# Channel mixing over the 896 tokens of two batches: pieces of 512 and 384 columns in place of two of 448

## Chip, cores and metric

One core of one Trainium2 chip. The metric is the device time of one execution in microseconds (us); shown is the median of several runs. The engines are TensorE (PE; its weight loads are listed apart as PEld), VectorE (DVE), ScalarE (ACT), GpSimd (POOL) and SyncE (SP), which issues most of the transfers.

## What is computed

The reference chains three parts on 2 batches of 448 tokens: attention (12 heads of 64), a gated feed-forward part that mixes tokens, and a last part that mixes tokens and then channels. The change is in the channel mixing of the last part (and in the tiles that lead to it):

```python
xt = x.transpose(0, 2, 1)                        # x: (2, 448, 768)
h = np.maximum(xt @ w_tok1, 0.0) @ w_tok2
u = x + h.transpose(0, 2, 1)
h2 = np.maximum(u @ w_ch1, 0.0) @ w_ch2          # w_ch1: 768 x 1536, w_ch2: 1536 x 768
return (u + h2).astype(np.float32)
```

## The kernel before

Activations are kept with channels on the 128 partitions and tokens along the columns, so that 768 channels are 6 tiles (`ND`) and the 1536 hidden channels are 12 (`NC`). Every number is held as a pair hi + lo of a rounded float32 (`F32R`) and its remainder. A product takes three matmuls, hi·hi, hi·lo and lo·hi (`three`), and each matmul has a weight load of its own.

The code records operations with the buffers that they read and write (`Plan.op`). `Plan.schedule` then simulates the engines with rough costs (one matmul over 448 columns is a slot of 203 ns, `SLOT`), picks at each step the operation that can start first, and so sets the order on each engine. `BUFS` says how many buffers each tag has; a buffer is given back when its last user is planned. One recorded PE operation is up to 6 matmuls (`mm`, `step=6`).

The last part goes in these steps:

- `tok1_unit`: 4 units, matmuls over 384 columns.
- `tok2_unit`: for batch `b` and channel tile `d` 6 matmuls over 448 columns into a bank (tag `gm`). DVE adds the bank to the residual (line L972), ACT casts the sum to hi (L350), DVE subtracts for lo (L367). The result `U[b][d]` is one tile `[128, 2, 448]` of tag `x` (12 buffers) that holds hi and lo of one batch.
- `ch1_unit`: for each of 12 hidden tiles `f`, first the 18 matmuls of batch 0 over 448 columns, then the 18 of batch 1, into the two banks of one `sc` buffer (there are 2 such buffers). `relu_split` reads both banks: ACT takes max(·, 0) as hi (L935), DVE the remainder as lo (L938).
- `ch2_unit`: for each of 6 output tiles `d` 36 matmuls over 448 columns for batch 0 and 36 for batch 1, each in a bank of its own. POOL has made hi + lo of `U[b][d]` ahead of time (`whole`, L891), DVE adds the bank to it (L1011), and a transfer writes it out (L1018). The last piece is cut into two halves, one issued by SP, the other by ACT.

All matmuls of these steps but the transposes are issued by one line, L274 in `mm`. The weights of each step come as 64-bit numbers through SP's queue (2 buffers of tag `r`), are turned into float32 by ACT and DVE (3 buffers of tag `t`), and are split into hi and lo by a cast (ACT, DVE, or POOL at L355) and a subtraction (DVE L367 or POOL L368) in buffers of tag `a`. There are 21 of these; in `ch2_unit` 18 hold the hidden tiles `f` from 3 on, and 3 hold weights, one `d` at a time.

Of the kernel before, what the change touches and what calls it, by code (L numbers as in the profile page):

```python
# [17 lines left out]
NP = H // 2  # L18
DM = H * D
ND = DM // 128  # L20
DF = 512
NF = DF // 128
ST = 112
NS = S // ST
NR = 3
# [42 lines left out]
    "ch1": (-24, 4),  # L68
    "ch2": (74, 5),
}  # L70
BUFS = {"x": 12, "v": 3, "q": 6, "a": 21, "r": 2, "t": 3, "h": 13, "p": 6, "gm": 4, "sc": 2, "sm": 4}
SLOT = 203.0
LAT = 140.0
EARLY = 72.0
# [16 lines left out]
        return self.ap[i]  # L91


class Op:
    __slots__ = ("ways", "key", "seq", "deps", "bufs", "new", "eng", "fn", "start", "end", "nbytes", "nwait")


class Plan:
# [5 lines left out]
    def op(self, ways, key, r=(), w=(), nbytes=0):  # L104

        o = Op()
        o.ways, o.key, o.seq, o.nbytes = ways, key, len(self.ops), nbytes
        o.deps, o.new = [], []
        o.bufs = list(dict.fromkeys(list(r) + list(w)))
        for b in o.bufs:  # L110
            if b.users == 0 and b.ap is None:
                o.new.append(b)
            b.users += 1
            write = any(b is x for x in w)
            if write or b.psum:
                o.deps += b.last_writers + b.readers
                if write:
                    b.last_writers, b.readers = [o], []
                else:
                    b.readers = [o]  # L120
            else:
                o.deps += b.last_writers
                b.readers.append(o)
        o.deps = list(dict.fromkeys(o.deps))
        self.ops.append(o)
        return o

    def schedule(self):
# [14 lines left out]
        for b in {b for o in ops for b in o.bufs if b.ap is not None and b.tag in free}:  # L143
            free[b.tag].pop()
        ready = defaultdict(list)

# [76 lines left out]
class Net:  # L223
    def __init__(self, tc, io, pool, ps, anycap=False):
        self.tc, self.nc, self.io, self.pool, self.ps, self.anycap = tc, tc.nc, io, pool, ps, anycap
        self.plan = Plan()
        self.key = 0.0


    def buf(self, tag, shape, dtype=F32):  # L230
# [351 lines left out]
    def normalise(self, n, A):  # L582
# [30 lines left out]
        for h, rows in ((0, LO), (1, UP)):  # L613
# [7 lines left out]
                1,  # L621
                kn,
            )
        x = self.buf("x", [128, 2, S], F32R)
# [55 lines left out]
    def attention_anycap(self, n):  # L680
# [10 lines left out]
        for h, r in ((0, LO), (1, UP)):  # L691
            for m in range(NS):
# [69 lines left out]
        x = self.buf("x", [128, 2, S], F32R)  # L762
        self.split(S, lambda: x[:, 0], lambda: x[:, 1], lambda: xf.ap, [xf], [x], k0 + 8)
        return x

# [194 lines left out]
            )  # L960
        return hi, lo

    def tok2_unit(self, h1, w2, x2, d):
# [9 lines left out]
        u = self.buf("x", [128, 2, S], F32R)  # L973
        self.split(S, lambda: u[:, 0], lambda: u[:, 1], lambda: z.ap, [z], [u])
        return u


    def ch1_unit(self, ws, U, f):
        ps = self.bank2()
        for b in range(B):  # L980
            terms = []
            for d in range(ND):
                n, c = divmod(f % 2 * ND + d, 4)
                cs = slice(c * 128, (c + 1) * 128)
                terms += self.three(
                    lambda i, n=n, cs=cs: ws[n][:, i, cs], lambda i, d=d, b=b: U[b][d][:, i], [ws[n], U[b][d]]
                )
            self.mm(ps, lambda b=b: ps[:, b, :S], terms, 1)
        hi, lo = (self.buf("q" if f < 3 else "a", [128, 2, S], F32R) for _ in range(2))
        self.relu_split(2 * S, (hi, lambda: hi.ap), (lo, lambda: lo.ap), ps, lambda: ps[:, :, :S])  # L990
        return [[hi, lo]] * B, lambda i, b: (hi, lo)[i][:, b]

    def ch2_unit(self, ws, h2, U, d):
        nc, io = self.nc, self.io
        for b in range(B):
            ps = self.bank()
            terms = []
            for f in range(NC):
                cs = slice(f % 4 * 128, (f % 4 + 1) * 128)
                terms += self.three(  # L1000
                    lambda i, f=f, cs=cs: ws[f // 4][:, i, cs], lambda i, f=f, b=b: h2[f][1](i, b), [ws[f // 4], *h2[f][0][b]]
                )
            self.mm(ps, lambda ps=ps: ps[:, :S], terms, 1)
            u = U[b][d]
            cuts = [slice(0, S // 2), slice(S // 2, S)] if (b, d) == (B - 1, ND - 1) else [slice(0, S)]
            o = [self.h([128, cs.stop - cs.start]) for cs in cuts]
            for i, cs in enumerate(cuts):
                self.whole(o[i], u, cs)
                self.dve(
                    cs.stop - cs.start,  # L1010
                    lambda o=o[i], ps=ps, cs=cs: nc.vector.tensor_tensor(out=o.ap, in0=ps[:, cs], in1=o.ap, op=ALU.add),  # L1011
                    [ps, o[i]],
                    [o[i]],
                )
            for i, (cs, out) in enumerate(zip(cuts, (nc.sync, nc.scalar))):
                self.load(
                    128 * (cs.stop - cs.start) * 4,
                    lambda o=o[i], b=b, cs=cs, out=out: out.dma_start(  # L1018
                        out=io["out"][b, d * 128 : (d + 1) * 128, cs], in_=o.ap
                    ),  # L1020
                    [],
                    [o[i]],
                    on="ACT" if i else "SP",
                )

    def run(self):
# [42 lines left out]
        for b in range(B):  # L1069
            h1[b] = stage([lambda t=t: self.tok1_unit(b, tr[b], xr, w1, t) for t in range(NT)], 4)  # L1070
        for b in range(B):
            U[b] = stage([lambda d=d: self.tok2_unit(h1[b], w2, x2[b], d) for d in range(ND)], 1.1)

        c1 = {}

# [84 lines left out]
def build(arrays):  # L1160
    import concourse.bacc as bacc

    nc = bacc.Bacc("TRN2", target_bir_lowering=False, num_devices=1)
    io = {
        n: nc.dram_tensor(f"{n}_in", a.shape, mybir.dt.from_np(a.dtype), kind="ExternalInput").ap()
        for n, a in arrays.items()
    }
    io["out"] = nc.dram_tensor("out_t", (B, DM, S), F32, kind="ExternalOutput").ap()
    with tile.TileContext(nc) as tc:
        program(tc, io)  # L1170
    return nc
# [10 lines left out]
```

## Time and profile before

| | |
|---|---|
| median of 3 runs | 442.62 us (442.54 to 443.59) |
| the profiled execution's own time | 444.11 us |
| its span in the trace | 442.3 us |
| PE busy | 427.0 us (97%) |
| DVE, ACT busy | 264.8 us (60%), 265.7 us (60%) |
| POOL busy | 105.5 us (24%) |
| first matmul of `ch1_unit` | at 257.44 us |
| first matmul of `ch2_unit` | at 346.73 us |
| matmuls in each of the two steps | 432 |

The profile is of one execution. Its own time is 1.8 us longer than the span that the trace covers. Matmuls overlap in the trace: one begins while the one before it still drains, so the time that a matmul takes from its engine is the distance from its start to the next one's start, not its duration.

### The profile page before, as it was taken

The page shows a single profiled execution, that of the slowest core. Times are in us where ns is not written, and L with a number is a line of the kernel's source. Part 1 is how long each engine was busy: PE and PEld are TensorE (multiplying, and loading weights), DVE is VectorE, ACT ScalarE, POOL GpSimd, SP SyncE. Part 2 cuts the span into 40 slices and gives each one's busy share as a digit, 9 for nine tenths or more (in the row PEclk, how much of TensorE's full clock was granted, in tenths as well). Part 3 has the DMA queues.
Part 4 walks back from the last instruction along what each step waited for, and adds up shares of the span by engine and source line. Part 5 has one row for each costly group of instructions (what it writes and reads, how often), then busy time and mean ns, then how long its engine had stood idle before and what let it go on. Part 6 is the DMA issues. An engine that isn't in the chain of part 4 may idle for free.

```text
span 442.3 us, 5467 instructions
## 1 busy us (share of the span) xinstructions
PE 427.0 (97%) x2050; PEld 350.2 (79%) x2050; DVE 264.8 (60%) x413; ACT 265.7 (60%) x386; POOL 105.5 (24%) x105
## 2 busy tenths in 40 slices
PE   8997989998999999999999999999999999999994
PEld 5553546566775889999999999999999999999993
DVE  4899989776665765896546899655202242344210
ACT  6998899999999567525537825775404333353100
POOL 0333342320100141567005473111010011011100
PEclk9999989999999999999999999999999999999998
DMA  7535546352120402202402105444201223533010
GB/s 266 207 125 173 176 128 210 102 157 88 47 70 2 142 5 92 83 1 99 139 1 96 48 1 168 164 144 142 96 0 49 96 90 116 184 117 123 34 44 29
DMA packets 14867, 44.84 MB, mean 101 GB/s; under 512 B 1904, under 2 KB 4208, under 8 KB 14832
## 3 DMA queue, kind: packets, MB, share of 16 engines
q1 hardware_dynamic: 14688, 44.30, 30.4%
q8 instruction: 18, 0.29, 0.3%
q14 instruction: 17, 0.14, 0.1%
q10 hardware_dynamic: 144, 0.11, 0.1%
HBM read 41.65 MB, written 2.75 MB: 100 GB/s over the span
## 4 chain that ended last, share of the span: by engine, by line
PE 78%; ACT 12%; DVE 7%; issue 2%; POOL 0%; DVEq 0%; POOLq 0%; ACTq 0%
PE gm L274 48%; PE sc L274 20%; PE gm L572 5%; ACT a L514 3%; ACT a L522 3%; PE sc L540 2%; DVE t L449 1%; DVE q L367 1%; PE sc L905 1%; ACT L768 1%; DVE t L438 1%; DVE h L592 1%; PE gm L561 1%; PE sc L342 1%; DVE h L616 1%
## 5 line engine op out<-in xcount | busy, mean ns | idle before, releaser
L274 PE MATMUL gm<-a,a 128*128 128x448 f32 (+1 forms) x556 | 115.2, 363 | 0.0
L274 PEld LDWEIGHTS gm<-a,a 128*128 128x128 f32 x556 | 102.8, 188 | 8.4
L274 PE MATMUL sc<-x,a 128*128 128x448 f32 x432 | 89.4, 368 | 0.0
L274 PEld LDWEIGHTS sc<-x,a 128*128 128x128 f32 x432 | 81.1, 188 | 8.2
L572 PE MATMUL gm<-a,v 128*128 128x448 f32 x144 | 61.8, 558 | 4.8 <-ACT a L522 2.8
L427 DVE SCALAR_TENSOR_TENSOR t<-r,t 128x512 int32<-128x512 int32 (+1 forms) x52 | 40.5, 782 | 30.1 <-ACT t L420 27.9
L274 PE MATMUL gm<-q,a 128*128 128x448 f32 x268 | 57.3, 367 | 0.0
L407 ACT ACTIVATE t<-r 128x512 uint16<-128x512 uint16 (+1 forms) x52 | 40.5, 784 | 25.3 <-DVE a L367 20.8
L396 ACT ACTIVATE r<-r 128x512 f32<-128x512 f32 (+1 forms) x58 | 38.9, 670 | 25.3 <-DMA r<-ch_in 23.1
L274 PEld LDWEIGHTS gm<-q,a 128*128 128x128 f32 x268 | 50.3, 188 | 4.7
L572 PEld LDWEIGHTS gm<-a,v 128*128 128x128 f32 x144 | 25.5, 191 | 29.6 <-issue 20.6
L368 POOL TENSOR_TENSOR a<-t,a 128x512 fp32r<-128x512 f32 x21 | 29.4, 1402 | 77.6 <-DVE a L351 73.7
L355 POOL TENSOR_SCALAR a<-t 128x512 fp32r<-128x512 f32 x19 | 12.2, 644 | 127.3 <-PE gm L274 71.9
L420 ACT ACTIVATE t<-r 128x512 f16<-128x512 f32 (+1 forms) x52 | 40.3, 774 | 0.0
L367 DVE TENSOR_TENSOR a<-t,a 128x512 fp32r<-128x512 f32 x35 | 24.6, 704 | 20.7 <-POOL a L355 20.1
L522 ACT ACTIVATE a<-a,acap 128x896 f32<-128x896 f32 x36 | 36.5, 1043 | 0.1
L514 ACT ACTIVATE a<-sc,qs 128x896 f32<-128x896 f32 x36 | 35.1, 1004 | 2.2 <-PE sc L540 2.2
L891 POOL TENSOR_TENSOR h<-x 128x448 f32<-128x448 f32 (+1 forms) x25 | 33.5, 1368 | 9.0 <-PE gm L274 6.1
L274 PE MATMUL gm<-x,a 128*128 128x448 f32 x144 | 31.0, 372 | 0.0
L938 DVE SCALAR_TENSOR_TENSOR a<-sc,a 128x896 fp32r<-128x896 f32 x9 | 9.8, 1092 | 33.3 <-ACT a L935 33.3
L274 PEld LDWEIGHTS gm<-x,a 128*128 128x128 f32 x144 | 27.1, 188 | 3.3 <-issue 1.0
L935 ACT ACTIVATE a<-sc 128x896 fp32r<-128x896 f32 x9 | 8.3, 920 | 32.7 <-PE sc L274 32.7
(97 smaller groups left out, 492.5 us busy)
## 6 DMA issues: line engine op xcount, KB each, us to landing
r<-ch_in SPq DMA_DIRECT2D x36, 512.0 KB, 3.3
r<-w_in_in SPq DMA_DIRECT2D x12, 512.0 KB, 3.9
q<-qk_in SPq DMA_DIRECT2D x11, 544.0 KB, 4.3
v<-va_in SPq DMA_DIRECT2D x12, 288.0 KB, 4.4
r<-w_out_in SPq DMA_DIRECT2D x6, 512.0 KB, 3.4
out_t<-h SPq DMA_DIRECT2D x11, 224.0 KB, 1.9
r<-tok_in SPq DMA_DIRECT2D x2, 512.0 KB, 3.4
t<-w_sg_in SPq DMA_DIRECT2D x4, 224.0 KB, 2.5
```

Of the source, the lines that this page charges most:

```text
L274: self.nc.tensor.matmul(view(), l, rr, start=(i + m == 0), stop=(i + m == n - 1))
L355: lambda: nc.gpsimd.tensor_scalar(out(), src(), 1.0, 0.0, ALU.mult, ALU.add),
L367: "DVE": ("DVE", n / 0.96 + 155, lambda: nc.vector.tensor_tensor(**args()), not psum),
L368: "POOL": ("POOL", n * 2.3 + 60, lambda: nc.gpsimd.tensor_tensor(**args()), True),
L396: lambda: nc.scalar.activation(raw[:, :, 1].bitcast(F32), raw[:, :, 1].bitcast(F32), AF.Copy, scale=2.0**-112),
L407: lambda: nc.scalar.activation(t.ap.bitcast(U16)[:, 0::2], raw.ap.rearrange("p n t -> p (n t)").bitcast(U16)[:, 1::4], AF.Copy, scale=2.0* ...
L420: lambda: nc.scalar.activation(t.ap.bitcast(F16)[:, 1::2], raw[:, :, 1].bitcast(F32), AF.Copy),
L427: lambda: nc.vector.scalar_tensor_tensor(out=t.ap, in0=raw[:, :, 1], scalar=3, in1=t.ap, op0=ALU.logical_shift_left, op1=ALU.bitwise_or),
L514: lambda: nc.scalar.activation(te.ap, sc[:, 0:nn, :S], AF.Tanh, scale=self.qs),
L522: lambda: nc.scalar.activation(te.ap, te.ap, AF.Exp, scale=self.acap),
L572: nc.tensor.matmul(A[h][:, :S], V[:, 3 * j + h : 3 * j + h + 2].rearrange("p c d -> p (c d)"), E[j][:, h], start=(j == 0), stop=(j == 2),)
L891: lambda: self.nc.gpsimd.tensor_tensor(out=out.ap, in0=parts(0), in1=parts(1), op=ALU.add),
```

## The change

The 896 tokens of both batches are one row of columns, cut into pieces of 512 and 384 (`WIDE`) where it was cut at the batches into 448 and 448. For this `U[0][d]` and `U[1][d]` become two parts (`Part`) of one tile `[128, 2, 896]` of tag `x`, of which there are 6 in place of 12; the x tiles of the attention, which have the same tag, are held in the same way. The first piece takes all of batch 0 and 64 columns of batch 1, so every matmul of `ch1_unit` in it needs both batches. The two pieces of `ch1_unit` lie next to each other in the two banks, and the hidden tiles are `[128, 896]`. The output in memory is `(768, 896)` in place of `(2, 768, 448)`.

```diff
+WIDE = slice(0, 512), slice(512, 2 * S)
...
-BUFS = {"x": 12, "v": 3, "q": 6, "a": 21, "r": 2, "t": 3, "h": 13, "p": 6, "gm": 4, "sc": 2, "sm": 4}
+BUFS = {"x": 6, "v": 3, "q": 6, "a": 21, "r": 2, "t": 3, "h": 13, "p": 6, "gm": 4, "sc": 2, "sm": 4}
...
+class Part(Buf):
+    def __init__(self, whole, cs):
+        self.whole, self.cs, self.tag, self.psum = whole, cs, None, False
...
+    @property
+    def ap(self):
+        return self.whole.ap[:, :, self.cs]
...
+    def x_part(self, d, b):
+        if b == 0:
+            self.both[d] = self.buf("x", [128, 2, B * S], F32R)
+        return Part(self.both[d], slice(b * S, (b + 1) * S))
...
     def ch1_unit(self, ws, U, f):
         ps = self.bank2()
-        for b in range(B):
+        for m, ts in enumerate(WIDE):
             terms = []
             for d in range(ND):
...
-                    lambda i, n=n, cs=cs: ws[n][:, i, cs], lambda i, d=d, b=b: U[b][d][:, i], [ws[n], U[b][d]]
-                )
-            self.mm(ps, lambda b=b: ps[:, b, :S], terms, 1)
-        hi, lo = (self.buf("q" if f < 3 else "a", [128, 2, S], F32R) for _ in range(2))
...
+                    lambda i, d=d, ts=ts: U[0][d].whole[:, i, ts],
+                    [ws[n], U[0][d], U[1][d]],
+                )
+            size = ts.stop - ts.start
+            self.mm(ps, lambda m=m, size=size: ps[:, m, :size], terms, size / S)
+        hi, lo = (self.buf("q" if f < 3 else "a", [128, 2 * S], F32R) for _ in range(2))
+        src = lambda: ps.ap.rearrange("p m n -> p (m n)")[:, : 2 * S]
...
     def ch2_unit(self, ws, h2, U, d):
         nc, io = self.nc, self.io
-        for b in range(B):
+        for m, ts in enumerate(WIDE):
...
-                self.whole(o[i], u, cs)
+                at = slice(ts.start + cs.start, ts.start + cs.stop)
+                parts = lambda i, at=at: U[0][d].whole.ap.bitcast(F32)[:, i, at]
+                self.gps(
+                    size // n * 2.3 + 60,
+                    lambda o=o[i], parts=parts: nc.gpsimd.tensor_tensor(out=o.ap, in0=parts(0), in1=parts(1), op=ALU.add),
+                    [U[0][d], U[1][d]],
+                    [o[i]],
+                )
```

Up to the last matmul of `tok2_unit` the order of the instructions on PE is that of before. From there the planner's order differs. In the rows below the number behind a name tells buffers apart: `sc` is the bank pair of one hidden tile, `x` an input tile of `ch1_unit`, `a` a weight, `h` a residual or an output tile, and `gm` a bank of `tok2_unit`.

PE at the start of `ch1_unit`, before (x_2292 to x_2362 are batch 0, x_2372 to x_2425 batch 1):

```order
L274 MATMUL sc_2416<-x_2292,a_2155 128x448 x3
L274 MATMUL sc_2416<-x_2307,a_2155 128x448 x3
L274 MATMUL sc_2416<-x_2320,a_2155 128x448 x3
L274 MATMUL sc_2416<-x_2324,a_2155 128x448 x3
L274 MATMUL sc_2416<-x_2360,a_2175 128x448 x3
L274 MATMUL sc_2416<-x_2362,a_2175 128x448 x3
L274 MATMUL sc_2416<-x_2372,a_2155 128x448 x3
L274 MATMUL sc_2416<-x_2395,a_2155 128x448 x3
L274 MATMUL sc_2416<-x_2400,a_2155 128x448 x3
L274 MATMUL sc_2416<-x_2410,a_2155 128x448 x3
L274 MATMUL sc_2416<-x_2414,a_2175 128x448 x3
L274 MATMUL sc_2416<-x_2425,a_2175 128x448 x3
```

The same place in the changed kernel (x_2286 to x_2349 are the six tiles of both batches, sc_2399 is the first hidden tile and sc_2421 the second):

```order
L303 MATMUL sc_2399<-x_2286,a_2149 128x512 x3
L303 MATMUL sc_2399<-x_2301,a_2149 128x512 x3
L303 MATMUL sc_2399<-x_2313,a_2149 128x512 x3
L303 MATMUL sc_2399<-x_2324,a_2149 128x512 x3
L303 MATMUL sc_2421<-x_2286,a_2169 128x512 x3
L303 MATMUL sc_2421<-x_2301,a_2169 128x512 x3
L303 MATMUL sc_2421<-x_2313,a_2194 128x512 x3
L303 MATMUL sc_2421<-x_2324,a_2194 128x512 x3
L303 MATMUL sc_2399<-x_2337,a_2169 128x512 x3
L303 MATMUL sc_2399<-x_2349,a_2169 128x512 x3
L303 MATMUL sc_2399<-x_2286,a_2149 128x384 x3
L303 MATMUL sc_2399<-x_2301,a_2149 128x384 x3
```

The first hidden tile's matmuls on the channel tiles 4 and 5 (x_2337, x_2349) now stand behind twelve matmuls of the second hidden tile; before, all of the first hidden tile came first, batch by batch.

DVE at the end of `tok2_unit`, batch 1, before (the rows with `gm` are the sums, those with `x` the lo parts; the lo part of channel tile 0 of batch 1 stands one row above):

```order
L972 TENSOR_TENSOR h_1886<-gm_2350,h_1886 128x448
L972 TENSOR_TENSOR h_1891<-gm_2364,h_1891 128x448
L972 TENSOR_TENSOR h_1900<-gm_2376,h_1900 128x448
L972 TENSOR_TENSOR h_1934<-gm_2387,h_1934 128x448
L972 TENSOR_TENSOR h_1945<-gm_2402,h_1945 128x448
L367 TENSOR_TENSOR x_2395<-h_1886,x_2395 128x448
L367 TENSOR_TENSOR x_2400<-h_1891,x_2400 128x448
L367 TENSOR_TENSOR x_2410<-h_1900,x_2410 128x448
L367 TENSOR_TENSOR x_2414<-h_1934,x_2414 128x448
L367 TENSOR_TENSOR x_2425<-h_1945,x_2425 128x448
```

The same place in the changed kernel, from the lo part of channel tile 0 of batch 1 on:

```order
L396 TENSOR_TENSOR x_2286<-h_1858,x_2286 128x448
L1001 TENSOR_TENSOR h_1880<-gm_2342,h_1880 128x448
L1001 TENSOR_TENSOR h_1885<-gm_2355,h_1885 128x448
L1001 TENSOR_TENSOR h_1894<-gm_2366,h_1894 128x448
L396 TENSOR_TENSOR x_2301<-h_1880,x_2301 128x448
L396 TENSOR_TENSOR x_2313<-h_1885,x_2313 128x448
L396 TENSOR_TENSOR x_2324<-h_1894,x_2324 128x448
L1001 TENSOR_TENSOR h_1928<-gm_2378,h_1928 128x448
L1001 TENSOR_TENSOR h_1939<-gm_2390,h_1939 128x448
L396 TENSOR_TENSOR x_2337<-h_1928,x_2337 128x448
L396 TENSOR_TENSOR x_2349<-h_1939,x_2349 128x448
```

The lo parts of the channel tiles 1 to 3 moved ahead of the sums of 4 and 5.

POOL in this stretch, before (rows with `a` are lo parts of weights, rows `h<-x` the sums hi + lo for `ch2_unit`):

```order
L368 TENSOR_TENSOR a_2231<-t_2180,a_2231 128x512
L891 TENSOR_TENSOR h_2310<-x_2292 128x448
L368 TENSOR_TENSOR a_2334<-t_2271,a_2334 128x512
L891 TENSOR_TENSOR h_2357<-x_2307 128x448
L891 TENSOR_TENSOR h_2385<-x_2320 128x448
L891 TENSOR_TENSOR h_2397<-x_2372 128x448
L891 TENSOR_TENSOR h_2412<-x_2324 128x448
```

The same place in the changed kernel:

```order
L397 TENSOR_TENSOR a_2225<-t_2174,a_2225 128x512
L397 TENSOR_TENSOR a_2327<-t_2265,a_2327 128x512
L1046 TENSOR_TENSOR h_2374<-x_2286 128x512
L1046 TENSOR_TENSOR h_2386<-x_2286 128x384
L1046 TENSOR_TENSOR h_2408<-x_2301 128x512
L1046 TENSOR_TENSOR h_2418<-x_2301 128x384
L1046 TENSOR_TENSOR h_2460<-x_2313 128x512
```

The sums hi + lo begin one row later and now go tile by tile over both batches, 512 columns and then 384, where the first four of before were of x_2292, x_2307, x_2320 (batch 0) and x_2372 (batch 1). On SP the transfers stand in the order of before: for each output tile one output, one weight, one output, two weights.

## Rows read from the trace of the kernel before

**Rows 1.** The profile's page: busy time of each engine; relu_split's two groups.

```profile
PE 427.0 (97%) x2050; PEld 350.2 (79%) x2050; DVE 264.8 (60%) x413; ACT 265.7 (60%) x386; POOL 105.5 (24%) x105
...
L938 DVE SCALAR_TENSOR_TENSOR a<-sc,a 128x896 fp32r<-128x896 f32 x9 | 9.8, 1092 | 33.3 <-ACT a L935 33.3
...
L935 ACT ACTIVATE a<-sc 128x896 fp32r<-128x896 f32 x9 | 8.3, 920 | 32.7 <-PE sc L274 32.7
```

**Rows 2.** The chain that ended last, from 225 us: start, us, what.

```profile
257.61 89.28 PE sc L274 x432
346.89 89.29 PE gm L274 x432
```

**Rows 3.** Busy time by windows, ch1_unit and ch2_unit: window, its length, each engine's busy us.

```profile
257.44:346.73 89.29, 89.29 (x434) 81.08 (x433) 46.53 (x58) 41.35 (x61) 17.76 (x15) 1.00 0.31 101
346.73:436.00 89.27, 89.27 (x433) 80.89 (x431) 25.96 (x40) 25.23 (x37) 9.33 (x15) 1.00 0.27 94
```

**Rows 4.** Timeline of PE in four dense stretches: start, us, engine line operation, count.

```profile
145.67 11.27 PE L274 MATMUL gm<-a,x 128*128 128x512 f32 x49
...
194.71 10.50 PE L274 MATMUL gm<-a,a 128*128 128x448 f32 x51
...
232.69 9.52 PE L274 MATMUL gm<-a,a 128*128 128x384 f32 x54
...
257.65 88.61 PE L274 MATMUL sc<-x,a 128*128 128x448 f32 x428
```

**Rows 5.** Groups by form in such stretches: busy us, mean ns of one, idle before.

```profile
L274 PE MATMUL gm<-a,x 128*128 128x512 f32 x46 | 10.6, 389 | 0.0
...
L274 PE MATMUL gm<-a,a 128*128 128x448 f32 x51 | 10.5, 365 | 0.0
...
L274 PE MATMUL gm<-a,a 128*128 128x384 f32 x54 | 9.5, 334 | 0.0
...
L274 PE MATMUL sc<-x,a 128*128 128x448 f32 x428 | 88.6, 368 | 0.0
...
L274 PEld LDWEIGHTS gm<-a,a 128*128 128x128 f32 x53 | 9.2, 188 | 0.0
```

**Rows 6.** Timeline of PE, DVE and POOL around the end of tok2_unit.

```profile
242.57 15.04 PE L274 MATMUL gm<-q,a 128*128 128x448 f32 x72
...
248.26 1.69 DVE L367 TENSOR_TENSOR x<-h,x 128x448 fp32r<-128x448 f32 x3
...
254.68 2.35 DVE L972 TENSOR_TENSOR h<-gm,h 128x448 f32<-128x448 f32 x4
257.64 0.62 DVE L972 TENSOR_TENSOR h<-gm,h 128x448 f32<-128x448 f32 x1 [0.62 <-PE gm L274]
...
258.72 5.10 DVE L367 TENSOR_TENSOR x<-h,x 128x448 fp32r<-128x448 f32 x4
...
254.84 2.29 POOL L891 TENSOR_TENSOR h<-x 128x448 f32<-128x448 f32 x2 [1.10 <-DVE x L367]
258.88 9.88 POOL L891 TENSOR_TENSOR h<-x 128x448 f32<-128x448 f32 x7 [1.76 <-DVE x L367]
```

**Rows 7.** ch2_unit: timelines of PE, POOL and DVE at one output tile; POOL's waits.

```profile
369.05 2.02 PE L274 MATMUL gm<-q,a 128*128 128x448 f32 x9
...
376.49 2.02 PE L274 MATMUL gm<-q,a 128*128 128x448 f32 x9
...
371.83 0.62 POOL L355 TENSOR_SCALAR a<-t 128x512 fp32r<-128x512 f32 x1 [9.29 <-PE gm L274]
...
372.49 0.69 DVE L367 TENSOR_TENSOR a<-t,a 128x512 fp32r<-128x512 f32 x1 [2.62 <-POOL a L355]
...
POOL a L355 <- PE gm L274: 71.9, 14, 18.0
```

**Rows 8.** The last output's two sums on DVE; the transfer of one half.

```profile
436.20 0.69 DVE L1011 TENSOR_TENSOR h<-gm,h 128x224 f32<-128x224 f32 x2 [6.81 <-PE gm L274]
...
out_t<-h SPq DMA_DIRECT2D x1, 112.0 KB, 2.8
```

More of the change, by code (lines that the diff above doesn't have):

```diff
@@ L91, in __getitem__ @@
         return self.ap[i]
+class Part(Buf):
+    def __init__(self, whole, cs):
+        self.whole, self.cs, self.tag, self.psum = whole, cs, None, False
+        self.users, self.end = 0, 0.0
+        self.last_writers, self.readers = [], []
+    @property
+    def ap(self):
+        return self.whole.ap[:, :, self.cs]
 class Op:
@@ L109, in op @@
         o.bufs = list(dict.fromkeys(list(r) + list(w)))
-        for b in o.bufs:
-            if b.users == 0 and b.ap is None:
+        held = []
+        for b in list(o.bufs):
+            if isinstance(b, Part):
+                held.append(b.whole)
+            elif b.users == 0 and b.ap is None:
                 o.new.append(b)
@@ L123, in op @@
                 b.readers.append(o)
+        for b in dict.fromkeys(held):
+            if b.users == 0:
+                o.new.append(b)
+            b.users += 1
+            o.bufs.append(b)
         o.deps = list(dict.fromkeys(o.deps))
@@ L142, in schedule @@
         free = {t: [0.0] * n for t, n in BUFS.items()}
-        for b in {b for o in ops for b in o.bufs if b.ap is not None and b.tag in free}:
+        for b in {b for o in ops for b in o.bufs if b.tag in free and b.ap is not None}:
             free[b.tag].pop()
@@ L227, in __init__ @@
         self.key = 0.0
+        self.both = {}
     def buf(self, tag, shape, dtype=F32):
@@ L961, in tok1_unit, with tok2_unit @@
         return hi, lo
-    def tok2_unit(self, h1, w2, x2, d):
+    def tok2_unit(self, b, h1, w2, x2, d):
         nc = self.nc
@@ L1000, in ch2_unit @@
                 terms += self.three(
-                    lambda i, f=f, cs=cs: ws[f // 4][:, i, cs], lambda i, f=f, b=b: h2[f][1](i, b), [ws[f // 4], *h2[f][0][b]]
+                    lambda i, f=f, cs=cs: ws[f // 4][:, i, cs], lambda i, f=f, ts=ts: h2[f][i][:, ts], [ws[f // 4], *h2[f]]
                 )
[L1003 to L1006, printed above, removed]
+            self.mm(ps, lambda ps=ps, size=size: ps[:, :size], terms, size / S)
+            n = 2 if (m, d) == (1, ND - 1) else 1
+            cuts = [slice(i * size // n, (i + 1) * size // n) for i in range(n)]
+            o = [self.h([128, size // n]) for _ in cuts]
             for i, cs in enumerate(cuts):
-                self.whole(o[i], u, cs)
+                at = slice(ts.start + cs.start, ts.start + cs.stop)
[6 more added lines that the diff above has]
+                )
                 self.dve(
-                    cs.stop - cs.start,
+                    size // n,
                     lambda o=o[i], ps=ps, cs=cs: nc.vector.tensor_tensor(out=o.ap, in0=ps[:, cs], in1=o.ap, op=ALU.add),
@@ L1015, in ch2_unit @@
             for i, (cs, out) in enumerate(zip(cuts, (nc.sync, nc.scalar))):
+                at = slice(ts.start + cs.start, ts.start + cs.stop)
                 self.load(
[L1017 to L1020, printed above, removed]
+                    128 * size // n * 4,
+                    lambda o=o[i], at=at, out=out: out.dma_start(out=io["out"][d * 128 : (d + 1) * 128, at], in_=o.ap),
                     [],
@@ L1071, in run @@
         for b in range(B):
-            U[b] = stage([lambda d=d: self.tok2_unit(h1[b], w2, x2[b], d) for d in range(ND)], 1.1)
+            U[b] = stage([lambda d=d: self.tok2_unit(b, h1[b], w2, x2[b], d) for d in range(ND)], 1.1)
         c1 = {}
@@ L1167, in build @@
     }
-    io["out"] = nc.dram_tensor("out_t", (B, DM, S), F32, kind="ExternalOutput").ap()
+    io["out"] = nc.dram_tensor("out_t", (DM, B * S), F32, kind="ExternalOutput").ap()
     with tile.TileContext(nc) as tc:
```

14 lines of the change are left out of this document (8 added, 6 removed).

## The prediction

> **What bounds the kernel now.** I read the page first: PE is busy for 427.0 of 442.3 us, and the other engines for 60% or less [rows 1]. A PE that is busy need not be at its best, so the chain that ended last comes next. From 257.6 us to the end it is PE alone, first the matmuls of `ch1_unit`, then those of `ch2_unit`, 432 of each [rows 2]. The windows over these two steps show PE busy for 89.29 of 89.29 and 89.27 of 89.27 us at a granted clock of 1.00, while DVE is busy for half of the first window and less of the second [rows 3]. So 178.56 us of the span are 864 matmuls without a gap, 206.67 ns each. The change acts there: it leaves their number as it is and alters how many columns each has. The question is what a matmul of 512 columns and one of 384 cost beside two of 448.
>
> The trace of before has all three sizes. Starts that follow each other without a gap give the interval: busy time of a dense stretch, less the duration of its last matmul, over the count less one.
>
> - 512 columns (the gated part): (11.27 - 0.389) / 48 = 226.7 ns
> - 384 columns (`tok1_unit`): (9.52 - 0.334) / 53 = 173.3 ns
> - 448 columns in `ch1_unit`: (88.61 - 0.368) / 427 = 206.7 ns
> - 448 columns in the gated part's output: (10.50 - 0.365) / 50 = 202.7 ns [rows 4, 5]
>
> From 384 to 512 the interval rises by 53.4 ns over 128 columns, 0.417 ns for each. A straight line between them passes 448 at 200.0 ns. The 448-column matmul lies above it, by 2.7 ns in one stage and by 6.7 ns in the stage that is changed. I don't know why; the argument needs only that this is so.
>
> **The matmuls.** A pair costs 2 x 206.67 = 413.3 ns now and 226.7 + 173.3 = 400.0 ns by the rows of its sizes. There are 432 pairs (12 hidden tiles x 18, 6 output tiles x 36): 432 x 13.3 ns = **-5.76 us**. Since PE has no gap in this stretch and nothing runs behind it but the last output, all of that comes off the end if PE stays without gaps. The bounds: were none of the 6.7 ns a matter of size, the gain would be 0; a gain above 5.76 would need a size to run faster than any row of it.
>
> A rule of the Trainium skill speaks against this sum. Its page "TensorE: Matmul & The Clock Gate", section "Back-to-back issue gap", gives the warm gap as columns over 2.4 plus 2.5 ns, a straight line with the same constant at each size; by it 512 and 384 are 215.8 + 162.5 = 378.3 ns and two of 448 also 378.3 ns, so the change would give nothing. Here the rows differ from the page in the constant (13 to 20 ns) and in the line: 448 lies off it. The rows decide, and I go by them.
>
> **The start of `ch1_unit`.** Before, its first 18 matmuls needed batch 0 alone, which was ready long ago, and batch 1 came 3.7 us later. Now the second row on PE needs batch 1 too. The planner answers by running channel tiles 0 to 3 of the first hidden tile, then tiles 0 to 3 of the second, and only then tiles 4 and 5. Nothing else is queued behind on PE that could run, and all after it would shift by the stall.
>
> When is each input needed? `ch1_unit` can start at 257.44 us, and a matmul of the first piece takes 0.227 us, so the lo part of tile 3 is read by the 11th matmul at 259.7, that of tile 4 by the 26th at 263.1, that of tile 5 by the 29th at 263.8. When is it there? `tok2_unit` runs 72 matmuls from 242.57 to 257.44, six for a tile, so tile 3 of batch 1 ends at 255.0 and its sum on DVE can start 0.2 us later, at 255.2 (the last sum followed the last matmul as closely: 257.64 after 257.44) [rows 6]. Sums follow each other in 0.58 us (four in 2.35, less the tail of the last) [rows 6]; so the lo parts of tiles 1 to 3, which stand directly behind this sum in the new order, start at 255.8. A lo part takes 0.54 us when POOL is idle (three in 1.69, less the tail of the last) and 1.5 us while POOL makes its sums hi + lo (the last three of the four that start at 258.72) [rows 6].
>
> - POOL idle: three x 0.54, done by 257.4, 2.3 us ahead. The two sums and the last two lo parts are done by 260. No stall.
> - POOL against every one of them, and with 512 columns in its passes (1.5 x 512 / 448 = 1.7 us each, an estimate): tile 3 at 260.9, a stall of 1.2; then two sums and two lo parts until 265.4, against 263.8 + 1.2: another 0.4. In all 1.6 us.
>
> POOL can make its first sum only when channel tile 0 of batch 1 is split, and has 7 sums behind it without a rest in the rows of before, so the truth lies between. Its first two passes, 1.3 and 1.0 us by the columns, fall mostly beside DVE's sums, which read a bank and took 0.58 us at 254.68, while POOL ran its own passes from 254.84 [rows 6]. That leaves two or three lo parts at 1.5 us: tile 3 near 259.5, tile 5 near 263.7. I take **0**, and keep 1.6 us as the upper end.
>
> **Weights in `ch2_unit`.** Three buffers hold its weights, and POOL refills one when PE has read it for the last time; 14 of POOL's waits there are for PE [rows 7]. Before, weight 0 is read last 12 matmuls into the second piece, 369.05 + 2.48 = 371.5; the cast starts at 371.83, the lo part ends at 372.49 + 0.69 = 373.2, and PE reads it at 376.49: 3.3 us to spare. The distance between the two reads is 24 matmuls of the second piece, 4.96 us before and 24 x 0.1733 = 4.16 now: 2.5 us to spare. For weights 1 and 2 it is 4.80 and 5.44 us. Cost **0**; without that slack each of five tile changes would stall by what is missing.
>
> **The rest at nothing.** `relu_split` takes 0.92 on ACT and 1.09 us on DVE [rows 1]; at the start the second and first hidden tile are interleaved, the first ends 9.9 us after 257.4, and its banks are wanted again at 14.4 us: 4.5 us for 2.0 us of work. POOL's sums hi + lo are made a whole step ahead of their use. One output tile of 512 or 384 columns in place of 448 is one transfer as before, in the same place of SP's queue, and only the last ones show: two halves of 192 columns in place of 224, with the sums at 0.69 us together and a transfer of 112 KB that takes 2.8 us to land [rows 8]. By columns the two sums save some 0.07 us and the transfer perhaps as much; I leave both out. Six x tiles in place of twelve cover the same memory, and up to `ch1_unit` PE's order is unchanged.
>
> **The sum.** 442.30 - 5.76 = 436.5 us of span for an execution like the profiled one, or 438.35 by its own time of 444.11. The median of the runs, 442.62, is 1.49 below that own time, so the same step gives 442.62 - 5.76 = **436.9 us**.
>
> **The rivals.**
> - *The surplus belongs to the stage.* The 448-column matmul takes 206.7 here and 202.7 ns elsewhere, so something other than size plays a part. If the 4.0 ns between them stick to every matmul of these steps, a pair is 408.0 ns and the gain 432 x 5.3 = 2.3: 440.3 us. If all 6.7 ns do, a pair is 413.3 and nothing is gained: 442.6 us. By the straight line of that page of the Trainium skill the time would be this too. For it: two values at one size. Against: 512 and 384 show one value each over 48 and 53 intervals, though the rows are from different stages, the 384 directly ahead of `tok2_unit`.
> - *Slower: the short matmul waits for its weights.* Each matmul has a weight load of 188 ns [rows 5]. 448 columns outlast it, 384 wouldn't. If the load must end before the next matmul starts, with the 13.3 ns that the line leaves beyond its slope, a piece of 384 takes 201.3 ns and a pair 428.0: +6.3 us, 448.9 us. It decides from 186.7 ns for the piece of 384 on. Against: `tok1_unit` runs 384 columns at 173.3 ns with loads of the same 188 ns, so loads overlap.
> - *The stall takes the gain.* It has an upper end of 1.6 us, so this alone gives 438.5 at most; it is part of my range.
>
> **Chances.** My forecast 0.82, with the range from its own bounds: up by the stall's 1.6 us and 0.1 for the spread of runs, down by 0.7 for the tail left out and a run below the median: 436.2 to 438.6. The stage's surplus 0.12, halved: 0.06 at 440.3 and 0.06 at 442.6, the straight line's result. Weight loads 0.03, other ways to be slower 0.03. About 0.3% (1.3 us) is what a measurement of this kernel can tell from no change, so 440.3 still counts as faster: 0.82 + 0.06 = 0.88. No change: 0.06 + 0.01 = 0.07. Slower: 0.05.
>
> **What would show it.** Right: in the changed kernel the dense stretches of `ch1_unit` and `ch2_unit` show 226.7 and 173.3 ns between starts, the two steps last 172.8 us together, and PE is idle for less than 1.6 us near 259 to 264 us, ended by a lo part of tile 3 or 5 on DVE. Wrong: the intervals keep 4 to 7 ns above these values (the stage's surplus), the 384 columns fall to 188 ns or more (loads), or PE has gaps at each of the output tiles, ended by a weight's lo part (the 2.5 us used up).

## The result, and the profile after

| | before | after |
|---|---|---|
| median, runs on one chip by turns (4 each) | 442.98 us (442.54 to 443.59) | 438.83 us (438.21 to 439.35) |
| the profiled execution's own time | 444.11 us | 438.43 us |
| its span | 442.3 us | 436.7 us |
| `ch1_unit` + `ch2_unit` in the chain | 178.57 us | 173.99 us |

The ratio is 0.9905 (95%: 0.9884 to 0.9926): faster by 4.2 us (3.3 to 5.1). The forecast was 436.9 us with a range from 436.2 to 438.6; the median lies 0.2 us above the range. The direction was right, the gain was forecast too large.

The page of the changed kernel, busy time of each engine [rows 1]: PE lost 5.2 us, its weight loads 5.9, DVE 1.9.

```profile
PE 421.8 (97%) x2050; PEld 344.3 (79%) x2050; DVE 262.9 (60%) x413; ACT 265.9 (61%) x387; POOL 104.8 (24%) x104
```

The chain that ended last, the two rows that answer to [rows 2]:

```profile
255.92 87.17 PE sc L303 x432
343.09 86.82 PE gm L303 x432
```

And the windows over these two steps [rows 3]; the columns are length, busy time of PE, PEld, DVE, ACT and POOL, granted clock, DMA share, GB/s:

```profile
255.92:343.09 87.17, 87.17 (x434) 78.25 (x433) 46.05 (x57) 41.75 (x62) 19.49 (x17) 1.00 0.32 103
343.09:429.91 86.82, 86.81 (x433) 77.82 (x431) 26.11 (x40) 25.12 (x37) 9.37 (x15) 1.00 0.30 97
```

Three things are to be read here. PE is still without a gap, at the same granted clock (1.00, its 2.4 GHz level). The steps gave 2.11 and 2.47 us, 4.58 together, where 5.76 was forecast. And the two steps are no longer alike: the matmuls are the same in number and columns, yet `ch1_unit` takes 0.35 us more. The difference of the spans, 5.6 us, looks like the forecast 5.76 by chance. The execution that was profiled before entered `ch1_unit` 1.69 us later than this one, and such starts move from execution to execution: the chains of the experiments put this one between 255.6 and 256.9 us with the new layout and between 256.5 and 257.7 with the old one (less the added matmuls there), and the changed kernel alone has it at 255.92 in one profile and at 256.89 in another. After the last matmul it took 6.1 us to the end before, and 6.8 in the changed kernel.

Where the 1.18 us went is seen on the timeline of PE over the first output tile of `ch2_unit` (start, us, engine line operation, count). The first 9 matmuls of each piece have a row of their own, because their operand has another name (`q`).

```profile
342.93 2.24 PE L303 MATMUL gm<-q,a 128*128 128x512 f32 x9
345.01 6.28 PE L303 MATMUL gm<-a,a 128*128 128x512 f32 x27
351.13 1.75 PE L303 MATMUL gm<-q,a 128*128 128x384 f32 x9
352.72 4.84 PE L303 MATMUL gm<-a,a 128*128 128x384 f32 x27
357.40 2.24 PE L303 MATMUL gm<-q,a 128*128 128x512 f32 x9
```

From one start to the next, 27 matmuls of 512 columns take 351.13 - 345.01 = 6.12 us, 226.7 ns each, and 27 of 384 take 4.68 us, 173.3 ns each: to a tenth the intervals of [rows 4]. But the first 9 of a piece take 2.08 / 9 = 231.1 ns and 1.59 / 9 = 176.7 ns. The starts of the single records show the pattern, in ns from start to start at the beginning of a piece:

```
512 columns behind 384:  229 233 236 224 231 236 228 233 231 226 227 227 227 ...
384 columns behind 512:  170 175 178 185 176 181 174 173 173 174 173 173 173 ...
```

A piece of 36 matmuls of 512 columns takes 8.201 us, 41 ns more than 36 x 226.67, and one of 384 takes 6.266 us, 26 ns more than 36 x 173.33. In the changed kernel there are 18 of each, 12 in `ch1_unit` and 6 in `ch2_unit`: 12 x 67 = 0.80 us and 6 x 67 = 0.40 us, 1.20 us together. Summed over the single records it is 0.77 and 0.40 us, 1.17 together, because the order at the start of `ch1_unit` has a piece of only six matmuls of 512 columns, and the 384 behind it lose 4 ns in place of 26. That is the missing 1.18 us and the 0.35 us between the steps.

### The profile page after: what moved, and what is told of

Its sections match the earlier page's. It is cut to its first block, busy times and chain, and to the rows that moved or that the text cites. A ratio compares the mean times of both kernels' runs of the same rounds, so it can differ in the third digit from the quotient of the medians.

```text
span 436.7 us, 5467 instructions
## 1 busy us (share of the span) xinstructions
PE 421.8 (97%) x2050; PEld 344.3 (79%) x2050; DVE 262.9 (60%) x413; ACT 265.9 (61%) x387; POOL 104.8 (24%) x104
## 4 chain that ended last, share of the span: by engine, by line
PE 75%; ACT 12%; DVE 10%; issue 2%; POOL 0%; DVEq 0%; POOLq 0%; ACTq 0%
PE gm L303 48%; PE sc L303 20%; PE gm L601 3%; ACT a L543 3%; ACT a L551 3%; DVE t L478 2%; DVE h L621 1%; PE sc L569 1%; DVE q L396 1%; ACT L797 1%; PE sc L934 1%; DVE t L467 1%; DVE h L645 1%; ACT t L449 1%; ACT t L436 1%
## 5 line engine op out<-in xcount | busy, mean ns | idle before, releaser
L303 PE MATMUL gm<-a,a 128*128 128x384 f32 (+2 forms) x556 | 113.1, 359 | 0.0
L303 PEld LDWEIGHTS gm<-a,a 128*128 128x128 f32 x556 | 100.6, 188 | 8.6
L303 PE MATMUL sc<-x,a 128*128 128x512 f32 (+1 forms) x432 | 87.3, 363 | 0.0
L303 PEld LDWEIGHTS sc<-x,a 128*128 128x128 f32 x432 | 78.3, 188 | 9.0
L303 PE MATMUL gm<-q,a 128*128 128x448 f32 (+2 forms) x268 | 57.0, 366 | 0.0
L397 POOL TENSOR_TENSOR a<-t,a 128x512 fp32r<-128x512 f32 x20 | 28.3, 1415 | 71.5 <-DVE a L380 60.3
L303 PE MATMUL gm<-a,x 128*128 128x512 f32 x108 | 26.4, 401 | 0.0
```

Of the source, the lines that this page charges most:

```text
L303: self.nc.tensor.matmul(view(), l, rr, start=(i + m == 0), stop=(i + m == n - 1))
L397: "POOL": ("POOL", n * 2.3 + 60, lambda: nc.gpsimd.tensor_tensor(**args()), True),
```

## The experiments

There are ten runs. What stood open after the result: whether the cost at the changes of size is what was lost (theory), or something of the new layout and order took it (a rival); and why 448 columns cost 206.7 ns in these steps and 202.7 ns in the gated part [rows 4], since that decides how much of the gain belongs to the sizes 512 and 384. All kernels with added matmuls write them to a bank that nothing reads.

**after_again** is the changed kernel once more.

> The changed kernel once more, for a narrower ratio. The trace of the changed kernel has the two steps of channel mixing at 173.99 us (87.17 + 86.82) where before had 178.57, so 4.58 us less; stages ahead of them are the same on PE. Theory (the sum was 1.2 us too high because matmuls of a new size settle only after 6 to 9 of them, and nothing else changed): the time falls by 4.6 us, ratio 0.9897, and the two steps again take 174.0 us. Rival (something ahead of channel mixing costs time as well, from the x tiles of double size): the time falls by 4.1 us or less while the two steps take 174.0.

Measured: 439.37 us (5 runs) against 443.5 (23 runs), ratio 0.9900 (0.9881 to 0.9918), 4.4 us; the chain's rows are again 87.17 and 86.82 us. The 95% interval reaches from 3.6 to 5.3 us, so the times alone don't separate the theory's 4.6 from the rival's 4.1; that layout_448 below, which has the same double tiles ahead of channel mixing, isn't slower than before speaks against the rival. Over all runs, before has a median of 443.49 us in 53 and after 439.22 in 9. The 442.62 from which the forecast was made, a median of three runs, lay 0.9 below that.

**layout_448** keeps the layout of the changed kernel and, as far as its rows at the end of `tok2_unit` show, the order, and cuts the pieces at 448 again. Not every wait stays: a first piece of 448 columns is batch 0 alone, and POOL's first sum hi + lo starts at 249.26 us, where the changed kernel's waits for batch 1 until 252.07. PE waits for nothing in these steps in either kernel.

```diff
-WIDE = slice(0, 512), slice(512, 2 * S)
+WIDE = slice(0, S), slice(S, 2 * S)
...
-        src = lambda: ps.ap.rearrange("p m n -> p (m n)")[:, : 2 * S]
-        self.relu_split(2 * S, (hi, lambda: hi.ap), (lo, lambda: lo.ap), ps, src)
+        two = lambda t: t.ap.rearrange("p (m n) -> p m n", m=2)
+        self.relu_split(2 * S, (hi, lambda: two(hi)), (lo, lambda: two(lo)), ps, lambda: ps[:, :, :S])
```

> The changed kernel with pieces of 448 and 448: tiles of both batches, waits for both batches and the planner's new rules stay, the sizes are those of before. Theory (all of the gain is a matter of size): the two steps take 178.6 us and the time is that of before within 0.3%. Rival (tiles or order contribute, either way): the two steps take 178.6 us and the time differs from before by 1 us or more.

Measured: 442.8 us (12 runs) against 443.5 (23), ratio 0.9989 (0.9979 to 1.0). The chain of this kernel:

```profile
255.64 89.28 PE sc L303 x432
344.92 89.29 PE gm L303 x432
```

These are the durations of [rows 2] to 0.01 us. So in these steps the layout and the order give nothing and take nothing; the sizes do it all. The 0.7 us between the medians lies outside the steps and at the edge of what the runs can tell from nothing.

**snake** tests the cost of a change of size: every second tile runs its pieces in the reverse order, so that equal sizes meet. Its records have 20 changes between the two sizes, where the changed kernel's have 35 (36 with the one from the 448 columns of `tok2_unit`).

```diff
-        for m, ts in enumerate(WIDE):
+        for m, ts in list(enumerate(WIDE))[:: 1 if f % 2 else -1]:
...
-        for m, ts in enumerate(WIDE):
+        for m, ts in list(enumerate(WIDE))[:: 1 if d % 2 else -1]:
```

> The changed kernel with every second hidden tile and every second output tile taken in the other order of pieces, so that a piece is followed by one of its own size: 20 changes of size in place of 36. Theory (settling, about 41 ns for each change to 512 and 25 ns for each to 384 by the trace of the changed kernel): 10 x 41 + 10 x 25 = 0.66 us of settling in place of 1.19, the two steps 173.4 to 173.5 us, 0.5 us below the changed kernel; steady intervals 226.7 and 173.3 as there. Rival (the missing 1.2 us is spread over all matmuls of the stage): 174.0 us.

Measured: 438.31 us (5 runs), ratio to before 0.9883 (0.9864 to 0.9902). Its chain, and PE's timeline at the second and third output tile:

```profile
256.44 86.87 PE sc L303 x432
343.31 86.62 PE gm L303 x432
```

```profile
349.38 2.24 PE L303 MATMUL gm<-q,a 128*128 128x512 f32 x9
351.47 6.28 PE L303 MATMUL gm<-a,a 128*128 128x512 f32 x27
357.59 2.20 PE L303 MATMUL gm<-q,a 128*128 128x512 f32 x9
359.63 6.28 PE L303 MATMUL gm<-a,a 128*128 128x512 f32 x27
```

At 349.38 the 512 columns follow 384: 2.09 us for the first nine. At 357.59 they follow 512 and take 2.04 us, the settled 226.7 ns each. It is the change of size that costs, not the first matmuls of a bank or a tile. The steps take 173.49 us, 0.50 less than in the changed kernel; over the single records, what lies above the settled intervals fell from 1.17 to 0.67 us, the same 0.50. This is the fastest of the ten by its median; beside after_again (439.37) the medians of five runs each are 1.1 us apart, of which the trace accounts for 0.5.

**alternate** goes the other way: `ch1_unit` runs three matmuls of 512 and three of 384 by turns.

```diff
-        for m, ts in enumerate(WIDE):
...
+        for d in range(ND):
...
+                for m, ts in enumerate(WIDE):
+                    for t, (k, i) in enumerate(THREE):
+                        self.nc.tensor.matmul(
+                            ps[:, m, : ts.stop - ts.start],
+                            ws[n][:, k, cs],
+                            U[0][d].whole[:, i, ts],
...
```

> The changed kernel with the pieces of 512 and 384 taken in turn in the hidden tiles, three matmuls of the one and three of the other, 144 changes of size in place of 24 in that step. Theory (settling after each change, the first three intervals behind a change as in the changed kernel: 229, 233, 236 and 171, 175, 177 ns): 407 ns a pair, 87.9 us for the step where the changed kernel has 87.17. Rival (the loss at a change is a cost of its own, 41 and 25 ns each time): 216 x 400 + 72 x 66 ns = 91.2 us.

Measured in a single run: `ch1_unit` 88.08 us in the chain.

```profile
256.88 88.08 PE sc L1016 x432
```

Were each change a fixed price, the 144 changes here against 24 in the changed kernel's `ch1_unit` would cost 120 x 33 ns = 4.0 us; the step is 0.91 us longer than 87.17. The records show triples of 233 236 224 or 229 234 235 ns for 512 columns and of 175 174 175 or 169 177 185 for 384, on average 16 and 7.5 ns above three settled ones: 72 x 23.5 ns = 1.7 us over 216 x 400 ns = 86.4 us. What is paid lies on the matmuls behind a change, a few ns each, for as long as they haven't settled.

**before_512_first** asks after the 206.7 ns: the kernel before, with 12 unread matmuls of 512 columns between `tok2_unit` and `ch1_unit`.

```diff
+                if f == 0:
+                    ps, w, u = self.bank(), c1[0], U[1][0]
+                    self.mm(ps, lambda: ps.ap, [(lambda: (u[:, 0, 0:128], w[:, 0]), [u, w])] * 12, 512 / 448, step=12)
```

> The kernel before with 12 matmuls of 512 columns, whose result nobody reads, between the token mixing and the channel mixing. Theory A (448 columns have two states, and what was run ahead decides: 202.7 ns after 512 columns, as after the gated part's 512, and 206.7 after 384): the two steps take 864 x 202.7 = 175.1 us, 3.5 less, the added matmuls cost 2.8, so the time falls by 0.7 us. Theory B (206.7 belongs to these steps or to the size in them): the two steps stay at 178.6 us, and the time rises by 2.8 us.

Measured: 442.91 us (12 runs) against 443.5 (23), ratio 0.9988 (0.9975 to 1.0001), with the added matmuls' 2.8 us in it. The chain:

```profile
259.69 87.55 PE sc L274 x432
347.25 87.57 PE gm L274 x432
```

The same 864 matmuls of 448 columns as in [rows 2] now take 175.12 us, 202.7 ns each, 3.45 us less. So the 4.0 ns are no property of the stage and none of the size: this stage runs 448 columns at 202.7 ns, too, if something else ran ahead.

**before_one_512** adds a single such matmul.

```diff
+                if f == 0:
+                    ps, w, u = self.bank(), c1[0], U[1][0]
+                    self.mm(ps, lambda: ps.ap, [(lambda: (u[:, 0, 0:128], w[:, 0]), [u, w])], 512 / 448)
```

> The kernel before with one matmul of 512 columns, whose result nobody reads, ahead of channel mixing. Twelve of them brought the 864 matmuls of 448 columns behind them from 206.7 to 202.7 ns. Theory A (the state at 448 columns is set by the size of the matmul just ahead, one is enough): the two steps take 175.1 us, the added matmul 0.2, the time falls by 3.2 us. Theory B (it takes several that have settled): 178.6 us, the time rises by 0.2 us.

Measured: 443.73 us (11 runs) against 443.55 (15), ratio 1.0002 (0.9991 to 1.0012).

```profile
256.73 89.27 PE sc L274 x432
346.00 89.29 PE gm L274 x432
```

One is not enough: after a few intervals of 202 to 206 ns the matmuls are back at 206.7.

**primers** and **primers_reset** put unread matmuls of another size ahead of each of the 12 hidden tiles of the kernel before, the first with six each of 512, 384, 496, 256, 480, 416, 500, 320, 464, 128, 504 and 432 columns, the second with a list that returns to 128 columns between the sizes.

```diff
     def ch1_unit(self, ws, U, f):
+        z, w, u, n0 = self.bank(), ws[0], U[1][0], PRIME[f]
+        self.mm(z, lambda: z[:, :n0], [(lambda: (u[:, 0, 0:128], w[:, 0, :n0]), [u, w])] * 6, n0 / 448)
```

> The kernel before with 6 unread matmuls of another size ahead of each of the 12 hidden tiles: 512, 384, 496, 256, 480, 416, 500, 320, 464, 128, 504, 432 columns in this order. It shows the interval of the 36 matmuls of 448 columns behind each. Theory A (two states at 448, set by what ran last): 202.7 ns behind 512 and 206.7 behind 384, as seen so far; behind the other sizes one of the two, the larger sizes like 512 and the smaller ones like 384. Theory B (the state is set once and then stays): all twelve at 202.7, from the first on. Were any at 200.0, two pieces of 448 would be as good as 512 and 384.

> The kernel before with unread matmuls ahead of the hidden tiles, 6 of 128 columns ahead of every second one: 12 x 512, 6 x 128, 6 x 256, 6 x 128, 1 x 496, 6 x 128, 6 x 416, 6 x 128, 6 x 320, 6 x 128, 1 x 256, 6 x 384. Six of 128 brought the 448-column matmuls from 202.7 to 206.7 ns in the run primers, so each other size is now tried from there. Theory A (what ran last decides): 206.7 behind each 128, 202.7 behind the 12 of 512. Which of the others flip it is open: in the run primers one size, 496, did it from 206.7, while 256, 416 and 320 were only tried from 202.7. Theory B (only sizes over 448 flip it): 202.7 behind 512 and 496 alone.

Measured in a single run each. In primers the 448 columns settle at 206.7 ns behind 512, 384 and 128 columns and at 202.7 ns behind the nine other sizes; never at 200. Of these nine only 496 and 504 were tried from the upper value. In primers_reset the 448 columns settle at 202.7 behind twelve matmuls of 512, where six had left 206.7, and behind six of 128 now at 206.7, now at 202.7. Six of 256 and six of 416 brought them down from the upper value, so sizes below 448 do it, too, and theory B falls; a single one of 496 brought them up, and behind a single one of 256 and six of 384 they stayed up. Its timeline of PE at the first four tiles:

```profile
259.52 7.46 PE L275 MATMUL sc<-x,a 128*128 128x448 f32 x36
266.81 0.78 PE L275 MATMUL gm<-a,x 128*128 128x128 f32 x6
267.43 7.65 PE L275 MATMUL sc<-x,a 128*128 128x448 f32 x36
...
275.63 7.46 PE L275 MATMUL sc<-x,a 128*128 128x448 f32 x36
282.93 0.78 PE L275 MATMUL gm<-a,x 128*128 128x128 f32 x6
283.55 7.51 PE L275 MATMUL sc<-x,a 128*128 128x448 f32 x36
```

Both times 36 matmuls at the lower value (7.46 us) are followed by six of 128 columns; behind the first six the next 36 last 7.65 us and settle at the upper value, behind the second they last 7.51 and settle at the lower. So neither the size that ran last decides, nor that size with the value ahead of it. Something from further back may play a part, or the exact moment of the change, or chance; which, these runs don't say.

The trace of before shows the same ahead of `ch1_unit`, with 128-column transposes between two groups of twelve matmuls:

```profile
210.89 2.72 PE L274 MATMUL gm<-a,a 128*128 128x448 f32 x12
214.02 2.69 PE L274 MATMUL gm<-a,a 128*128 128x448 f32 x12
```

In the single records, each group stands behind six transposes. The first runs at the upper value (207 206 207 207 ns), the second at the lower (202 203 199 207), and the next 36, from 217.12 us on, at the upper again. So before had gone over to the upper value ahead of its 384 columns already, and these need not be what set it.

**sizes** measures the disputed price: the output tiles of `ch2_unit` are cut at 480, 496, 512, 504, 464 and 448 columns.

```diff
+FIRST = 480, 496, 512, 504, 464, 448
...
-        for m, ts in enumerate(WIDE):
+        for m, ts in enumerate((slice(0, FIRST[d]), slice(FIRST[d], 2 * S))):
```

> The changed kernel with other pieces in the six output tiles of the last step: 480 and 416, 496 and 400, 512 and 384, 504 and 392, 464 and 432, 448 and 448; each size has 36 matmuls, of which the last 20 should be settled. Theory A (a straight line, 0.4167 ns for each column and 13.3 ns, off which 448 alone lies by its state): 213.3 and 186.7, 220.0 and 180.0, 226.7 and 173.3, 223.3 and 176.7, 206.7 and 193.3 ns. Theory B (sizes of whole 128 columns lie on the line and the others above it, by up to 6.7 ns): only 512 and 384 on the line.

Measured in a single run; the rows of PE's timeline whose distance to the next start gives 27 settled intervals, with that next start:

```profile
353.18 5.20 PE L304 MATMUL gm<-a,a 128*128 128x416 f32 x27
358.22 2.18 PE L304 MATMUL gm<-q,a 128*128 128x496 f32 x9
360.24 6.19 PE L304 MATMUL gm<-a,a 128*128 128x496 f32 x27
366.27 1.78 PE L304 MATMUL gm<-q,a 128*128 128x400 f32 x9
367.88 5.02 PE L304 MATMUL gm<-a,a 128*128 128x400 f32 x27
372.75 2.23 PE L304 MATMUL gm<-q,a 128*128 128x512 f32 x9
...
389.26 6.28 PE L304 MATMUL gm<-a,a 128*128 128x504 f32 x27
395.38 1.76 PE L304 MATMUL gm<-q,a 128*128 128x392 f32 x9
396.97 4.98 PE L304 MATMUL gm<-a,a 128*128 128x392 f32 x27
401.79 2.06 PE L304 MATMUL gm<-q,a 128*128 128x464 f32 x9
```

For 416 columns (358.22 - 353.18) / 27 = 186.7 ns, and so on, to some 0.4 ns, since the view rounds to 0.01 us. The settled means of the single records, beside the line through 384 and 512 (0.4167 ns a column and 13.3 ns):

| columns | 384 | 392 | 400 | 416 | 432 | 448 | 464 | 480 | 496 | 504 | 512 |
|---|---|---|---|---|---|---|---|---|---|---|---|
| ns | 173.3 | 178.4 | 180.0 | 186.7 | 195.9 | 206.7 | 208.8 | 216.9 | 223.4 | 226.7 | 226.7 |
| above the line | 0 | 1.7 | 0 | 0 | 2.5 | 6.7 | 2.2 | 3.5 | 3.4 | 3.3 | 0 |

The 206.7 at 448 is the upper of its two values; the lower, 202.7, lies 2.7 above the line. Neither guess held: 448 is not the only size off the line, and not only multiples of 128 lie on it (400 and 416 do, too). Of the six ways to cut 896 columns none is below 512 + 384, 400.0 ns a pair: 480 + 416 and 496 + 400 take 403.5 and 403.4, the others 404.7 and more. The Trainium skill's page "TensorE: Matmul & The Clock Gate", section "Back-to-back issue gap", has one line for all sizes, with 2.5 ns where four sizes here have 13.3 and the others up to 20; by that line the change would have given nothing. The section gives this line for the gap of a single matmul by itself, which the prediction left out; for a stream in which each matmul has its weight load, as here, it gives about 131 ns at 512 columns. Neither agrees with the 226.7 ns measured here, and the measurement decides.

**pairs** carries snake on: the first pieces of two hidden tiles, then their second ones, in the order 384 384 512 512 512 512 384 384.

```diff
-        for m, ts in enumerate(WIDE):
+        for j, (m, ts) in enumerate(list(enumerate(WIDE))[:: 1 if f // 2 % 2 else -1]):
...
-            self.mm(ps, lambda m=m, size=size: ps[:, m, :size], terms, size / S)
+            self.mm(ps, lambda m=m, size=size: ps[:, m, :size], terms, size / S, self.key - f % 2 * 6.7 + j * 6.9)
```

> As the run snake, but two hidden tiles go together in the first step: the first piece of both, then the second piece of both, the next two the other way round, so that only 14 changes of size are left. Theory (41 and 25 ns of settling for each change): 7 x 41 + 7 x 25 = 0.46 us in place of 0.66, the two steps 173.3 us, 0.2 below snake and 0.7 below the changed kernel, as long as no bank pair comes late. Rival (the second tile of a pair waits for its banks, which relu_split gives back only 3 us before they are wanted): PE idle ahead of the third, fifth, ... hidden tile, ended by DVE or ACT, and the steps at 173.5 us or more.

Measured: 438.73 us (6 runs) against 443.46 (11), ratio 0.9902 (0.9882 to 0.9921), no better than snake. The changes settle as there, but a new wait stands at the start of `ch1_unit`, on PE's timeline and on DVE's:

```profile
256.72 5.02 PE L303 MATMUL sc<-x,a 128*128 128x384 f32 x28
261.96 4.42 PE L303 MATMUL sc<-x,a 128*128 128x384 f32 x20 [0.21 <-DVE x L396]
```

```profile
259.12 2.78 DVE L396 TENSOR_TENSOR x<-h,x 128x448 fp32r<-128x448 f32 x2
```

The lo part of tile 5 ends at 261.90 us, 5.18 after the first matmul; the matmul that reads it, the 29th, would have been due 4.9 us after the first, since 28 matmuls of 384 columns stand ahead of it. Two intervals, of 549 and 280 ns, lose 0.48 us there, more than the 0.26 that the fewer changes saved (12 in its records, 20 in snake). From first start to last start the two steps take 173.52 us in this kernel, 173.30 in snake, 173.80 in the changed one and 178.35 in the kernel before.

## Why the prediction went wrong, step by step

**The matmuls** are the step that failed, by its size. "432 pairs x 13.3 ns = -5.76 us" took the settled interval for every matmul. The settled intervals were right to a tenth of a ns, 226.7 and 173.3, but the sum lacks a term: the sizes change 36 times in these steps, 18 times to each size, and the matmuls behind a change together take some 41 and 26 ns too long before they settle. The prediction put this at nothing without a reason. By the records it is 1.17 us, and -5.76 + 1.17 = -4.59 against the measured -4.58. snake (20 changes, 0.50 us less) and alternate (a change after every three matmuls, 0.91 us more) show that it is this. The trace of before has such a change, too, at the gated part's first matmuls of 512 columns (behind a first interval of 548 ns 230 236 229 232 231 227); but the window from which I read 226.7 [rows 4] opened at the sixth matmul, and so left out all but one of them.

**The base** was too low. The forecast's 436.9 is 1.93 below the measured median. Settling is 1.18 of it, and the base 0.36 (442.62 against 442.98 in the comparison, 443.49 over all runs). The remaining 0.4 is within what the runs can tell, and I assign it to nothing. With either of the two put right, the median would have lain inside the range, so that it fell 0.2 us outside says less about the mechanism than the missing term does.

**The start of `ch1_unit`**, taken as 0 with an upper end of 1.6 us, was 0. PE's list of waits has none in these steps. Of the changed kernel, PE, DVE, then POOL [rows 6]:

```profile
255.76 87.33 PE L303 MATMUL sc<-x,a 128*128 128x512 f32 x432
```

```profile
254.02 2.97 DVE L396 TENSOR_TENSOR x<-h,x 128x448 fp32r<-128x448 f32 x3
256.91 1.14 DVE L1001 TENSOR_TENSOR h<-gm,h 128x448 f32<-128x448 f32 x2
258.16 2.80 DVE L396 TENSOR_TENSOR x<-h,x 128x448 fp32r<-128x448 f32 x2
```

```profile
252.07 2.28 POOL L1046 TENSOR_TENSOR h<-x 128x512 f32<-128x512 f32 x2 [2.47 <-DVE x L396]
254.91 10.31 POOL L1046 TENSOR_TENSOR h<-x 128x512 f32<-128x512 f32 x7 [0.56 <-DVE x L396]
```

The first matmul starts at 255.76. The lo part of tile 3 ends at 256.99, 1.23 us behind it, and is read at about 2.3; that of tile 5 ends 5.2 us behind and is read at about 6.4. The forecast had them 2.1 and 6.3 us behind the first matmul, about 1 us later than they came. The bounds were right to be set where they were: the three lo parts, two of them beside POOL's sums from 254.91 on, took 2.97 us, between the 1.6 of an idle POOL and the 5.1 of the worst case. In pairs this slack of 1.2 us is used up by the shorter pieces, and the stall of the prediction is there.

**Weights in `ch2_unit`**: forecast 2.5 us to spare for weight 0. Of the changed kernel, POOL and DVE at its first output tile [rows 7]:

```profile
353.49 0.62 POOL L384 TENSOR_SCALAR a<-t 128x512 fp32r<-128x512 f32 x1 [17.98 <-PE gm L303]
...
354.14 0.69 DVE L396 TENSOR_TENSOR a<-t,a 128x512 fp32r<-128x512 f32 x1 [2.12 <-POOL a L384]
```

The lo part ends at 354.83 and is read at 357.40: 2.57 us. This step was right.

**The rival of the short matmul that waits for its weights** fell: the settled 384 columns take 173.3 ns beside weight loads of 188. The groups by form over both steps:

```profile
L303 PE MATMUL gm<-a,a 128*128 128x384 f32 x162 | 29.0, 334 | 0.0
...
L303 PEld LDWEIGHTS gm<-a,a 128*128 128x128 f32 x324 | 58.6, 188 | 6.4
```

**The rival "the surplus belongs to the stage"** was wrong in what it would do to 512 and 384 columns, and had a true core. The 4.0 ns between the two values at 448 columns do not stick to the stage; they belong to a value that outlasts what ran ahead, and before_512_first takes them away without a change of size. So the gain has two parts: 864 x 4.0 ns = 3.46 us come from leaving that value, of which 512 and 384 columns showed no second one in any run here, and 432 x 5.3 ns = 2.30 us from 512 and 384 lying on the line where 448 at its better value lies 2.7 ns above it. Less 1.17 us of settling this is 4.59 us. Why 448 columns have two values, and what turns one into the other, was not found.

## What to carry to other kernels

Take a matmul's price from the starts of a dense stretch of its own size, not from a line through other sizes: here 448 columns lay 1.3 or 3.3% above the line, by what ran ahead. Where a cut makes sizes alternate, look at the first ten intervals behind a change apart from the rest, count the changes, and put equal sizes next to each other where no input is needed earlier by it. Compare steps inside the trace, not whole spans: here a start that came 1.7 us earlier made the span agree with a forecast that was 1.2 us wrong.

## What was not expected of the hardware

At an unchanged granted clock of 1.00 and with no wait, 864 matmuls of 448 columns took 178.57 us or 175.12, by what ran ahead of them. Six unread matmuls of 128 columns turned the lower value into the upper three times and twice did not; behind twelve of 512 came the lower, behind six or one the upper. Matmuls of 512 columns behind 384 need nine intervals until they settle and 384 behind 512 need six, at up to 12 ns more than settled for a matmul; 384 behind 448 need one (179, then 173 ns, in snake), and so not every change of size costs the same. And 504 columns cost as much as 512 (226.7 ns), 392 almost as much as 400 (178.4 and 180.0).
